# The planner's buffer numbers for conversion blocks, and no conversion beside the first units' thirds

## The chip, the cores and the metric

The kernel runs on one core of one Trainium2 chip, as one launch. The metric is the device time of that launch in microseconds (us). Inside the core five engines work in parallel, each in the order of its own queue: TensorE (PE, matrix products), VectorE (DVE), ScalarE (ACT), GpSimd (POOL) and SyncE (SP, which only issues transfers here). An engine whose next instruction must wait for a semaphore holds up everything behind it in its queue.

## The reference

Three layers follow each other on 2,304 tokens (4 batches of 576) with 512 features.

```python
# 1. attention in a sliding window of 64, 4 batches x 8 heads x 576 x 64
scores = where(0 <= i - j < 64, q @ k.T / 8, -1e9)
x = softmax(scores) @ v                       # -> (2304, 512)
# 2. eight experts; tokens are dealt out greedily by logit, 288 to an expert
order = np.argsort(-(x @ w_gate).flatten())
for idx in order:
    tok, e = divmod(idx, 8)
    if assigned[tok] < 0 and counts[e] < 288:
        assigned[tok] = e; counts[e] += 1
for e in range(8):
    out[assigned == e] = relu(x[assigned == e] @ w1[e]) @ w2[e]   # 512 -> 1024 -> 512
# 3. output network, 512 -> 2048 -> 512
h = out @ w_in
return maximum(0.01 * h, h) @ w_out
```

The inputs of the third layer, w_in and w_out, reach the chip as 32 blocks of 128 x 512 numbers of eight bytes each (512 KB a block), and the kernel itself rebuilds four-byte numbers from them.

## The kernel before, in words

**Stages.** The attention comes first (18 chunks of 128 tokens). Then the greedy dealing is done by a radix search in eight phases (class Router): each phase finds the tokens of one expert in a run of rounds. In a round TensorE counts with small matmuls into the tile rp, VectorE makes r_sat, and from the next rp it makes r_G and r_E for the following round. When a phase has its tokens (`ids`), GpSimd gathers their rows into xg, TensorE transposes them (tile xtp), and they are copied to xT and xF.

**Units.** The experts and the output network are one sequence of units, `Moe.seq`: expert 0, expert 1, output stage 0, experts 2 and 3, output stage 1, and so on. An expert has 8 units of 128 hidden features (units 0 to 7 are expert 0, 8 to 15 expert 1), an output stage has 16 (units 16 to 31 are the first). A unit i is made in two steps. `hstep(i)` is the product h, then ACT's relu into the tile hh. `ystep(i)` is the product with the second matrix, ya for an expert and oa for an output stage. The loop in `Moe.run` (lines 1153 on) queues hstep(i + 1) ahead of ystep(i). Expert 0 works straight from the loaded weights w_raw in float32; later units use weights split in two parts (a high part, cast by ACT, and a low part, by VectorE or GpSimd).

**The first units.** Expert 0's tokens come in three groups of 96. So that TensorE can begin before all have arrived, the products h0 and h1 are made by thirds: `third(i, a)` is 16 matmuls of 128 x 96 in four groups of four. After the third groups, `R.tick()` lets the driver of the routing queue more work. Only then is `hstep(0)` called, which finds all 12 groups done and queues the relu of h0.

**Conversion blocks.** Class Convert turns the 32 blocks into weights. A block is loaded by SP (or, once, by GpSimd) into the tile cv_in, which has four buffers: block n uses the buffer of block n − 4. So its transfer waits until block n − 4 has been used up. The first 18 blocks take three ACT passes and one step on VectorE, the *join*; the others two and two. A block that is kept on the chip is then cast by ACT into res, and VectorE makes its low part there.

**What sets the order.** All instructions are put into the queues by the program in one fixed order that a planner works out as the kernel is built. Class Clocks has a clock for each engine; Engine.call charges each instruction to it (so most operations after the attention have one line in the profile, L1303 before and L1309 after the change). A charged instruction starts when its inputs are written and when its output's buffer is free, and `Clocks.slot` says which buffer a tile lies in. `RouteDriver.tick` and `Convert.acts` and `piece` then ask these clocks whether a routing step or a conversion step fits. `Convert.there(n)` lets a block's first pass be queued once the planner thinks the block landed 400 ns ago. While `quiet` is set, neither passes nor joins are queued; `until(n)` still queues them when a weight is called for.

**The numbers of buffers.** The program's pool really gives block n buffer n mod 4. `Clocks.slot` numbers tiles of a kind in the order in which it meets them:

```python
k = self.ntag.get(t.tag, 0)
self.ntag[t.tag] = k + 1
self.slots[t.name] = t.tag, k % t.tag_meta.bufs
```

The clocks only start after the attention. They meet block 4 first (number 0), then 5, 6 and 3 (numbers 1, 2 and 3); then block 7, which is given number 0, and block 8, number 1. Block 7's transfer is thus charged as if it waited for block 4's buffer, where the pool has it wait for block 3's.

Of the kernel before, what the change touches and what calls it, by code (L numbers as in the profile page):

```python
# [1 line left out]

# [611 lines left out]
def make_pow2(nc, pool):  # L614
    out = []
    for r, (s, n) in enumerate(zip((25,) + SHIFTS, (127,) + NB)):
        w = pool.tile([128, 128], BF, name=f"pow2_{r}", tag=f"pow2_{r}")
        nc.gpsimd.memset(w, 0.0)
        a = 0 if n > 32 else 96
        nc.gpsimd.memset(w[a:a + n], float(1 << s))  # L620
        out.append(w)
    return out
# [30 lines left out]
class Convert:  # L653
# [24 lines left out]
            return self.st[n][:, :, 1].bitcast(F32)  # L678
        return self.pool.tile([128, 512], F32, tag="cv_r", name=f"cv_r{n}", bufs=NRING)
    def there(self, n):  # L680
        return self.done_at(self.st[n]) + 400 <= self.now()
    def open(self, n):

        if n not in self.out:
            while n not in self.st:
                self.load()
            self.out[n], self.left[n] = self.room(n), [2, 1, 0] if n < BYACT else [1, 0]
        t, o, act = self.st[n], self.out[n], self.nc.scalar.activation
        half = t.rearrange("p a b -> p (a b)").bitcast(F16).rearrange("p (a b) -> p a b", b=4)
        k = self.left[n].pop()  # L690
        if k == 0:
            act(o, t[:, :, 1].bitcast(F32), AF.Copy, scale=float(2.0 ** -112))
        elif k == 1:
            act(t[:, :, 0], t.bitcast(U8)[:, :, 3], AF.Copy, scale=1 / 32, bias=-31 / 64)
        else:
            act(half[:, :, 1], o, AF.Copy)
# [107 lines left out]
class Moe:  # L804
# [280 lines left out]
    def run(self):  # L1085
        nc, seq, R = self.nc, self.seq, self.route
        n = len(seq)
# [28 lines left out]
        self.split(0, 0)  # L1116
        self.split(1, 0)
        self.split(0, 1)
        def third(i, a):
            if a == 0:  # L1120
                self.ph[i] = self.pp.tile([128, 512], F32, tag="h", name=f"h{i}")
                self.hdone[i] = 12
            for k in range(4):
                nc.tensor.matmul(self.ph[i][:, 96 * a:96 * a + 96], self.w[i, 0][:, 128 * k:128 * k + 128], self.xF[a][:, k], start=(k == 0), stop=(k == 3), skip_group_check=True)
        for a in range(3):
            R.until(nc.done(self.xg[0, a]))
            self.xtrans(0, a)
            if a < 2:
                third(a, 0)
        for i, a in ((0, 1), (1, 1), (0, 2), (1, 2)):  # L1130
            third(i, a)
            R.tick()
        self.hstep(0)
        self.split(2, 0)
        self.split(1, 1)
        for i in range(n):
# [77 lines left out]
class Clocks:  # L1214
# [11 lines left out]
    def slot(self, ap):  # L1226

        t = ap.tensor
        if not hasattr(t, "tag_meta"):
            return None  # L1230
        if t.name not in self.slots:
            k = self.ntag.get(t.tag, 0)
            self.ntag[t.tag] = k + 1
            self.slots[t.name] = t.tag, k % t.tag_meta.bufs
        return self.slots[t.name]
    def cost(self, e, name, out, ins):
# [150 lines left out]
def build(nc, tc, qT, kT, v, vT, wg, cfd, cid, cbd, w12, wio, out):  # L1387
    with ExitStack() as ctx:
        ctx.enter_context(tc.manual_schedule())
        c = ctx.enter_context(tc.tile_pool(name="c", bufs=1))  # L1390
        dr = ctx.enter_context(tc.tile_pool(name="dr", bufs=1, space=bass.MemoryType.DRAM))
        iwg = c.tile([128, 256], F32, name="iwg")
        ident = iwg[:, :128]
        cft = c.tile([128, CFN], F32, name="cft")
        cit = c.tile([128, CIN], I32, name="cit")
        cbt = c.tile([128, CBN - MW - 128], BF, name="cbt")
        cf = {k: cft[:, o:o + n] for k, (o, n) in CFO.items()}
        ci = {k: cit[:, o:o + n] for k, (o, n) in CIO.items()}
        cb = {k: cbt[:, o - MW - 128:o - MW - 128 + n] for k, (o, n) in CBO.items() if o > MW}
        ones = c.tile([128, 128], BF, name="ones"); nc.vector.memset(ones, 1.0)  # L1400

        nc.scalar.activation(iwg[:, 0:1], ones[:, 0:1], AF.Exp)
        L = c.tile([128, 160], F32, name="L")[:, :NT * 8].rearrange("p (c e) -> p c e", e=8)
        xd = dr.tile([NTOK, DM], F32, name="xd")
        res = [c.tile([128, 2, 512], F32R, name=f"res_{n}") for n in range(NRES)]
        wsp = dr.tile([32 - NRES, 128, 1024], F32, name="wsp")
        cvp = ctx.enter_context(tc.tile_pool(name="cvp", bufs=1))
        cv = Convert(nc, cvp, wio, res)
        slow = cv.spare(CVA)
        def filler(i):  # L1410
            if i == -1:
                for _ in range(3):
                    cv.open(CVA)
                return
            if i is None:
                for _ in slow:
                    pass
                drain()
                return
            if queue and not next(queue[0], False):  # L1420
                queue.pop(0)
            if i == CV0:
                for _ in range(CVL):
                    cv.load()
            if i >= CV0 + 6:
                next(slow, None)
        rp = ctx.enter_context(tc.tile_pool(name="rp", bufs=1))
        rt = Router(nc, rp, None, L, cf, ci, cb, ones, make_pow2(nc, rp))
        rt.ident = ident
        ahead = {5: (0, 6), 11: (6, 12), 14: (12, 15), 17: (15, 18)}  # L1430
        queue = []
        def done(c):
            if c == 4:
                rt.start2()
            if c in ahead:
                queue.append(rt.ahead(*ahead[c]))
            if c == NT - 1:
                drain()
        def drain():
            while queue:  # L1440
                list(queue.pop(0))
        with tc.tile_pool(name="mk", bufs=1) as mk:
            maskb = mk.tile([128, MW + 128], BF, name="maskb")
            nc.scalar.dma_start(maskb, cbd[:, :MW + 128].bitcast(BF))
            wg_sb = iwg[:, 128:].rearrange("p (u e) -> p u e", u=4)
            def early():
                nc.scalar.dma_start(iwg, wg)
            def late():
                nc.sync.dma_start(cit, cid)
                nc.sync.dma_start(cft, cfd)  # L1450
                nc.sync.dma_start(cbt, cbd[:, MW + 128:].bitcast(BF))
                rt.start()
            attention(nc, tc, ident, maskb[:, MW:], qT, kT, v, vT, wg_sb, maskb, xd, L, filler, early, late, done)
        pa = ctx.enter_context(tc.tile_pool(name="m_pa", bufs=4, space=PSUM, reuse_waits="tile"))
        rt.pp = ctx.enter_context(tc.tile_pool(name="rps", bufs=1, space=PSUM, reuse_waits="tile"))
        pm = ctx.enter_context(tc.tile_pool(name="pm", bufs=1, space=PSUM, reuse_waits="tile"))
        rt.p0 = pm
        ph = ctx.enter_context(tc.tile_pool(name="m_ph", bufs=2, space=PSUM, reuse_waits="tile"))
        nc = cv.nc = rt.nc = Clocks(nc)
        nc.at["scalar"] = 7000.0  # L1460
        cv.side = nc.scalar.copy, nc.vector
        cv.now = lambda: max(nc.at["tensor"], nc.at["vector"])
        R = RouteDriver(nc, rt, cv)
        m = Moe(nc, tc, ctx, ident, pm, pa, ph, w12, wsp, xd, out, R)
        cv.relief = R.relief
        m.conv, m.warm = cv, cbt[:, :512]
        m.run()
# [25 lines left out]
```

## Time and profile before

| | us |
|---|---|
| device time, three runs | 774.66, 775.33, 775.5 |
| their median | 775.33 |
| the profiled execution: device time | 770.33 |
| the profiled execution: span of the trace | 768.7 |
| busy TensorE (PE) | 732.2 (95% of the span) |
| busy VectorE (DVE) | 440.3 (57%) |
| busy ScalarE (ACT) | 337.1 (44%) |
| busy GpSimd (POOL) | 165.6 (22%) |

The profile is of one execution, whose own device time is 770.33 us; the span runs from its first to its last recorded instruction. Times in the rows are us from the span's start. PE is TensorE's matmuls, PEld its loading of weights, which overlaps them. "[6.26 <-DMA cv_in<-in_wio_dram]" behind an instruction is the idle time of its engine before it and what ended it. SPq is SP's queue: an instruction there that lasts long is a transfer whose issue waits. In names of tiles the numbers are left out, so cv_in is any conversion block.

### The profile page before, as it was taken

What the parts mean: (1) busy time and instruction counts of PE and PEld (TensorE: products, weight loads), DVE (VectorE), ACT (ScalarE), POOL (GpSimd) and SP (SyncE); (2) the same over time, 40 slices, a digit from 0 to 9 for tenths busy, and PEclk for the clock granted to TensorE, in tenths of its full rate; (3) what the DMA queues carried; (4) which work ended last, traced back from release to release, by engine and by line L of the source; (5) the groups of instructions that cost most, each with busy time, mean ns of one, the idle gap of its engine ahead of it and who ended that gap; (6) DMA issues with size and microseconds to landing.
All of it is one profiled execution on the core that took longest, in us unless ns stands there. A gap on an engine that the chain in (4) does not pass through costs nothing.

```text
span 768.7 us, 14869 instructions
## 1 busy us (share of the span) xinstructions
PE 732.2 (95%) x5706; PEld 619.1 (81%) x5706; DVE 440.3 (57%) x1124; ACT 337.1 (44%) x761; POOL 165.6 (22%) x260
## 2 busy tenths in 40 slices
PE   6989567999999999999999999999999999999996
PEld 4767445798777799987777899888889998888895
DVE  3798884988998797875847823322233222222332
ACT  5898705577866444522122445222234532121321
POOL 6353130410100033010000288000038830000201
PEclk9999768999999999999999999999999999999999
DMA  9996156643785655261324363532436462324652
GB/s 358 416 416 260 49 192 222 201 161 110 253 290 213 237 198 187 84 251 55 132 88 165 105 214 131 216 109 86 163 108 224 138 219 82 110 87 162 245 184 91
DMA packets 39800, 138.55 MB, mean 180 GB/s; under 512 B 4783, under 2 KB 5679, under 8 KB 39729
## 3 DMA queue, kind: packets, MB, share of 16 engines
q1 hardware_dynamic: 34992, 122.62, 44.6%
q0 software_dynamic: 4448, 14.69, 5.5%
q8 instruction: 45, 0.74, 0.4%
q10 hardware_dynamic: 288, 0.30, 0.1%
q14 instruction: 27, 0.21, 0.1%
HBM read 117.66 MB, written 19.92 MB: 179 GB/s over the span
## 4 chain that ended last, share of the span: by engine, by line
PE 89%; DVE 7%; DMA 1%; ACT 1%; issue 1%; POOLq 0%; POOL 0%; SPq 0%; DVEq 0%; ACTq 0%
PE h L1303 39%; PE oa L1303 26%; PE ya L1303 14%; PE rp L1303 2%; PE ao L165 2%; PE as L130 1%; PE apt L150 1%; DVE amx L137 1%; PE xtp L1303 1%; DVE r_G L1303 1%; DMA cv_in<-in_wio_dram 1%; DMA aq<-in_q_dram 1%; PE warm L1303 1%; PE rq L1303 1%; ACT ap L145 1%
## 5 line engine op out<-in xcount | busy, mean ns | idle before, releaser
L1303 PE MATMUL h<-Y,w 128*128 128x512 f32 (+1 forms) x600 | 135.6, 372 | 0.0
L1303 PE MATMUL oa<-w,hh 128*128 128x512 f32 x540 | 134.9, 394 | 0.0
L1303 DVE SCALAR_TENSOR_TENSOR h<-h,tg 128x512 f32<-128x512 f32 (+1 forms) x80 | 51.5, 644 | 127.5 <-ACT tg L1303 127.2
L1303 PEld LDWEIGHTS h<-Y,w 128*128 128x128 f32 x600 | 104.0, 189 | 18.5
L1303 ACT COPY tg<-h 128x512 f32<-128x512 f32 (+1 forms) x80 | 43.7, 546 | 169.9 <-PE h L1303 160.1
L1303 PEld LDWEIGHTS oa<-w,hh 128*128 128x128 f32 x540 | 99.1, 188 | 19.5
L1303 PE MATMUL ya<-hh,w 128*128 128x288 f32 x672 | 101.0, 297 | 0.0
L1303 PE MATMUL h<-xT,w 128*128 128x288 f32 x672 | 100.8, 298 | 0.0
L1303 PEld LDWEIGHTS h<-xT,w 128*128 128x128 f32 x672 | 92.7, 188 | 0.6
L1303 PEld LDWEIGHTS ya<-hh,w 128*128 128x128 f32 x672 | 92.2, 188 | 0.0
L1303 POOL DMA_INDIRECT out_dram<-ot,sidx x18 | 18.9, 1050 | 310.0 <-DVE ot L1303 134.7
L1303 PE MATMUL h<-Y,res 128*128 128x512 f32 (+1 forms) x360 | 83.4, 375 | 0.0
L1303 PE MATMUL oa<-res,hh 128*128 128x512 f32 x324 | 82.3, 399 | 0.2 <-ACT hh L1303 0.2
L1303 POOL TENSOR_TENSOR w<-raw,w 128x512 fp32r<-128x512 f32 x48 | 60.4, 1295 | 95.4 <-ACT w L1303 95.0
L1303 DVE TENSOR_TENSOR hh<-h,hh 128x512 fp32r<-128x512 f32 (+1 forms) x80 | 51.0, 637 | 36.4 <-ACT hh L1303 33.5
L1303 PEld LDWEIGHTS h<-Y,res 128*128 128x128 f32 x360 | 62.3, 188 | 11.9
L1303 ACT CAST hh<-h 128x512 fp32r<-128x512 f32 (+1 forms) x80 | 43.6, 544 | 63.0 <-DVE h L1303 63.0
L1303 PEld LDWEIGHTS oa<-res,hh 128*128 128x128 f32 x324 | 59.4, 188 | 13.9 <-ACT hh L1303 1.2
L1303 ACT ACTIVATE hh<-h 128x288 fp32r<-128x288 f32 (+1 forms) x64 | 26.2, 411 | 87.9 <-PE h L1303 86.8
L1303 ACT CAST w<-raw 128x512 fp32r<-128x512 f32 x112 | 64.1, 621 | 0.0
L1303 DVE SCALAR_TENSOR_TENSOR hh<-h,hh 128x288 fp32r<-128x288 f32 x56 | 25.5, 456 | 64.5 <-ACT hh L1303 64.3
L1303 POOL DMA_INDIRECT xg<-xd,r_ids x24 | 24.1, 1005 | 127.5 <-issue 48.6
(181 smaller groups left out, 961.4 us busy)
## 6 DMA issues: line engine op xcount, KB each, us to landing
w<-wsp SPq DMA_DIRECT2D x80, 512.0 KB, 3.6
raw<-in_w_dram SPq DMA_DIRECT2D x53, 512.0 KB, 4.0
cv_in<-in_wio_dram SPq DMA_DIRECT2D x31, 512.0 KB, 4.5
wsp<-w SPq DMA_DIRECT2D x20, 512.0 KB, 3.1
avo<-in_v_dram SPq DMA_DIRECT2D x6, 876.0 KB, 9.8
aq<-in_q_dram SPq DMA_DIRECT2D x12, 384.0 KB, 9.7
avt<-in_vt_dram SPq DMA_DIRECT2D x6, 768.0 KB, 9.5
xd<-ax SPq DMA_DIRECT2D x18, 256.0 KB, 6.6
```

The source lines that it names most:

```text
L130: nc.tensor.matmul(S[64 * t:64 * t + 64, a, u, :].rearrange("p (b c) -> p b c", b=2), q[h], k[h], start=False, stop=True, skip_group_check ...
L137: nc.vector.tensor_reduce(out=mx, in_=S[:, a:a + n], axis=AX.X, op=ALU.max)
L145: nc.scalar.activation(p[:, u, :], S[:, a, u, :], AF.Exp, bias=nm[a][:, u:u + 1], scale=0.125)
L150: nc.tensor.transpose(pt[:, u, :], p[:, u, :], ident)
L165: nc.tensor.matmul(o[64 * t:64 * t + 64, h // 4, h % 4, :], ptb[:, u, 64 * t:64 * t + 64], (ve, vo)[t][m][:, s, h, :], start=True, stop=Tr ...
L1303: return f(*a, **kw)
```

## The change

The change has three parts. First, `Clocks.slot` takes a block's buffer from the number in its name, and at the start meets the tiles of the blocks already opened, so that they count. Second, `quiet` is set before the thirds of units 0 and 1 and is taken back after `hstep(0)`: in between no pass, no join and no load of a block is queued. Third, `there(n)` asks 4,000 ns in place of 400 for block 7 alone. No instruction's form changes; the rest of the order follows from the planner.

```diff
+import re
...
     def there(self, n):
-        return self.done_at(self.st[n]) + 400 <= self.now()
+        return self.done_at(self.st[n]) + (4000 if n == 7 else 400) <= self.now()
...
         self.split(0, 1)
+        self.conv.quiet = True
         def third(i, a):
...
             third(i, a)
             R.tick()
         self.hstep(0)
+        self.conv.quiet = False
         self.split(2, 0)
...
             k = self.ntag.get(t.tag, 0)
-            self.ntag[t.tag] = k + 1
+            m = re.match(r"cv_in(\d+)_", t.name)
+            if m:
+                k = int(m[1])
+            self.ntag[t.tag] = max(self.ntag.get(t.tag, 0), k + 1)
             self.slots[t.name] = t.tag, k % t.tag_meta.bufs
...
         nc = cv.nc = rt.nc = Clocks(nc)
+        for k in sorted(cv.out):
+            nc.slot(cv.out[k])
         nc.at["scalar"] = 7000.0
```

**ACT at the relus of units 0 and 1.** These are ACT's instructions from the copies of expert 0's tokens on; hh0 is the relu of unit 0, and `cv_r7<-cv_in7` is the first pass of conversion block 7. Before:

```order
L1303 COPY xT0_1_2188<-xtp0_0_2189 128x384
L1303 COPY xF1_2209<-xtp0_1_2204 128x384
L1303 COPY xT0_0_2187<-xtp0_2_2237 128x384
L1303 ACTIVATE cv_r7_2253<-cv_in7_2248 128x512
L1303 ACTIVATE hh0_2271<-h0_2196 128x288
L1303 ACTIVATE hh1_2273<-h1_2212 128x288
L1303 CAST res_2_73<-cv_in4_1190 128x512
L1303 ACTIVATE cv_r6_2301<-cv_in6_2132 128x512
L1303 CAST res_3_74<-cv_in5_1193 128x512
L1303 ACTIVATE cv_in6_2132<-cv_in6_2132 128x512
L1303 ACTIVATE cv_in6_2132<-cv_r6_2301 128x512
L1303 ACTIVATE hh2_2353<-h2_2313 128x288
```

And now:

```order
L1309 COPY xT0_1_2188<-xtp0_0_2189 128x384
L1309 COPY xF1_2209<-xtp0_1_2204 128x384
L1309 COPY xT0_0_2187<-xtp0_2_2237 128x384
L1309 ACTIVATE hh0_2288<-h0_2196 128x288
L1309 ACTIVATE hh1_2290<-h1_2212 128x288
L1309 ACTIVATE cv_r6_2322<-cv_in6_2132 128x512
L1309 ACTIVATE cv_in6_2132<-cv_in6_2132 128x512
L1309 ACTIVATE cv_in6_2132<-cv_r6_2322 128x512
L1309 CAST res_2_73<-cv_in4_1190 128x512
L1309 ACTIVATE hh2_2368<-h2_2334 128x288
L1309 CAST res_3_74<-cv_in5_1193 128x512
L1309 ACTIVATE cv_r7_2437<-cv_in7_2327 128x512
```

The first pass of block 7 stood ahead of hh0 and now stands behind hh2 and the cast res_3; hh0 and hh1 follow the copies directly. The other two passes of block 7 come with it, and block 6's three passes now stand ahead of the cast res_2.

**VectorE beside the thirds and the first products of expert 0.** These are VectorE's steps behind the last copy of expert 0's tokens, into the rounds of the search for expert 1; cv_r3, cv_in4 and cv_in5 as outputs are the joins of blocks 3, 4 and 5, and res_2 and res_3 low parts. Before:

```order
L1303 SCALAR_TENSOR_TENSOR cv_r3_1778<-cv_r3_1778,cv_in3_1006 128x512
L1303 SCALAR_TENSOR_TENSOR r_sat_126<-rp16_2217,ones_66 127x8
L1303 SCALAR_TENSOR_TENSOR cv_in4_1190<-cv_in4_1190 128x512
L1303 SCALAR_TENSOR_TENSOR r_G1_128<-r_E_1_0_2202,rp17_2251,cft_63 128x18x31
L1303 SCALAR_TENSOR_TENSOR r_E_1_1_2265<-r_E_1_0_2202,rp17_2251,r_M_122 128x18
L1303 SCALAR_TENSOR_TENSOR cv_in5_1193<-cv_in5_1193 128x512
L1303 SCALAR_TENSOR_TENSOR r_sat_126<-rp18_2280,ones_66 31x8
L1303 SCALAR_TENSOR_TENSOR r_G0_127<-r_E_1_1_2265,rp19_2306,cft_63 128x18x31
L1303 SCALAR_TENSOR_TENSOR r_E_1_2_2310<-r_E_1_1_2265,rp19_2306,r_M_122 128x18
L1303 TENSOR_TENSOR res_2_73<-cv_in4_1190,res_2_73 128x512
L1303 TENSOR_TENSOR res_3_74<-cv_in5_1193,res_3_74 128x512
L1303 SCALAR_TENSOR_TENSOR r_sat_126<-rp20_2315,ones_66 31x8
```

And now:

```order
L1309 SCALAR_TENSOR_TENSOR r_sat_126<-rp16_2217,ones_66 127x8
L1309 SCALAR_TENSOR_TENSOR r_G1_128<-r_E_1_0_2202,rp17_2248,cft_63 128x18x31
L1309 SCALAR_TENSOR_TENSOR r_E_1_1_2255<-r_E_1_0_2202,rp17_2248,r_M_122 128x18
L1309 SCALAR_TENSOR_TENSOR r_sat_126<-rp18_2261,ones_66 31x8
L1309 SCALAR_TENSOR_TENSOR r_G0_127<-r_E_1_1_2255,rp19_2286,cft_63 128x18x31
L1309 SCALAR_TENSOR_TENSOR r_E_1_2_2298<-r_E_1_1_2255,rp19_2286,r_M_122 128x18
L1309 SCALAR_TENSOR_TENSOR cv_r3_1778<-cv_r3_1778,cv_in3_1006 128x512
L1309 SCALAR_TENSOR_TENSOR cv_in4_1190<-cv_in4_1190 128x512
L1309 SCALAR_TENSOR_TENSOR r_sat_126<-rp20_2302,ones_66 31x8
L1309 SCALAR_TENSOR_TENSOR r_G1_128<-r_E_1_2_2298,rp21_2332,cft_63 128x18x31
L1309 SCALAR_TENSOR_TENSOR r_E_1_3_2337<-r_E_1_2_2298,rp21_2332,r_M_122 128x18
L1309 TENSOR_TENSOR res_2_73<-cv_in4_1190,res_2_73 128x512
```

The joins of blocks 3 and 4 moved behind two rounds of the search (r_sat, r_G, r_E), to the place after r_E_1_2, and the join of block 5 one round further. The load of block 7 is queued on SP behind the join of block 3, and moves with it.

## Rows read from the trace of the kernel before

**Rows 1.** The page: the span and the busy time of the engines.

```profile
span 768.7 us, 14869 instructions
...
PE 732.2 (95%) x5706; PEld 619.1 (81%) x5706; DVE 440.3 (57%) x1124; ACT 337.1 (44%) x761; POOL 165.6 (22%) x260
```

**Rows 2.** Waits of TensorE: engine, tile, line, releaser; us in total, times, longest.

```profile
PE rp L1303 <- DVE r_OB L1303: 4.8, 1, 4.8
PE ya L1303 <- ACT hh L1303: 4.1, 1, 4.1
...
PE oa L1303 <- ACT hh L1303: 0.2, 1, 0.2
```

**Rows 3.** The chain that ended last, 110 to 126 us: start, us, what.

```profile
112.37 6.76 DMA cv_in<-in_wio_dram
...
119.71 0.40 ACT hh L1303
```

**Rows 4.** Timeline, 111 to 131 us: start, us, engine, what, idle before and releaser.

```profile
112.37 18.85 SPq L1303 DMA_DIRECT2D cv_in<-in_wio_dram  x5
...
114.08 1.95 PE L1303 MATMUL h<-xT,w_raw 128*128 128x96 f32 x16
...
119.15 0.66 ACT L1303 ACTIVATE cv_r<-cv_in 128x512 f32<-128x512 f32 x1 [6.26 <-DMA cv_in<-in_wio_dram]
...
120.16 1.33 PE L1303 MATMUL ya<-hh,w_raw 128*128 128x288 f32 x2 [4.12 <-ACT hh L1303]
```

**Rows 5.** Busy time in stretches: us, PE, PEld, DVE, ACT, POOL, clock, DMA share, GB/s.

```profile
118.00:120.00 2.00, 0.00 (x0) 0.00 (x0) 0.00 (x0) 0.85 (x2) 0.00 (x0) 0.50 1.02 418
...
122.00:124.00 2.00, 2.00 (x5) 1.35 (x6) 0.97 (x3) 1.95 (x3) 0.00 (x0) 0.50 0.00 0
...
126.00:128.00 2.00, 2.00 (x10) 1.42 (x10) 1.49 (x4) 0.27 (x1) 0.00 (x0) 1.00 0.88 334
```

**Rows 6.** Timeline of TensorE: the starts of h2, ya of unit 1, h3.

```profile
124.92 0.65 PE L1303 MATMUL h<-xT,w_raw 128*128 128x288 f32 x2
...
127.53 0.65 PE L1303 MATMUL ya<-hh,w_raw 128*128 128x288 f32 x2
...
130.15 0.65 PE L1303 MATMUL h<-xT,w_raw 128*128 128x288 f32 x2
```

**Rows 7.** Timeline of one routing round, TensorE and VectorE.

```profile
126.45 0.17 PE L1303 MATMUL rp<-r_sat,pow 128*128 128x8 bf16 x1
...
126.69 0.81 DVE L1303 SCALAR_TENSOR_TENSOR r_G<-r_E,rp,cft 128x558 bf16<-128x558 f32 x1 [0.45 <-PE rp L1303]
...
127.56 0.69 DVE L1303 SCALAR_TENSOR_TENSOR cv_r<-cv_r,cv_in 128x512 int32<-128x512 int32 x1
...
128.68 0.18 DVE L1303 TENSOR_TENSOR_SCAN r_sat<-rp,ones 31x8 bf16<-31x8 f32 x1 [0.43 <-PE rp L1303]
...
129.07 0.17 PE L1303 MATMUL rp<-r_sat,pow 128*128 128x8 bf16 x1
```

**Rows 8.** Tile cv_in, 85 to 140 us: ns min/median/max by operation; load to landing.

```profile
L1303 ACT ACTIVATE cv_in<-cv_in x15: 649/708/1382, 89.3 to 136.6; 128x512 int32<-128x512 uint8 x7, 128x512 f32<-128x512 f32 x4, 128x512 f16<-128x512 f32 x4
...
DMA to landing us min/median/max: 3.4/3.5/6.8
```

**Rows 9.** Tile w_raw, issued by POOL from 108.3 to 108.6 us.

```profile
L1303 POOL DMA_DIRECT2D w_raw<-in_w_dram x1: 594/594/594, 108.4 to 108.4; - x1
...
DMA to landing us min/median/max: 6.2/6.2/6.2
```

**Rows 10.** Busy time in two stretches (columns as in rows 5).

```profile
114.90:122.00 7.10, 2.98 (x33) 2.34 (x32) 0.00 (x1) 2.85 (x7) 0.00 (x0) 0.71 0.81 329
184.00:281.00 97.00, 96.97 (x528) 76.23 (x527) 85.88 (x203) 59.12 (x110) 4.06 (x6) 1.00 0.64 223
```

**Rows 11.** Timeline, 286 to 304 us: gather of routing phase 3, its transposes.

```profile
288.45 0.92 POOL L1303 DMA_INDIRECT xg<-xd,r_ids  x1 [0.30 <-issue]
...
303.34 0.82 PE L1303 MATMUL xtp<-iwg,xg 96*128 96x96 f32 x8
```

## The prediction

> **What bounds the kernel now.** Four views were read, from coarse to fine. The page gives the span and TensorE's share: 768.7 us, TensorE busy for 95% of it [rows 1]. So what TensorE waits for is nearly all that can be won, and the list of its waits is next. There two waits stand out after the attention stage [rows 2]: 4.8 us behind r_OB, inside routing phase 0, which the change does not touch, and 4.1 us of the product ya behind ACT's hh, once. The chain of waits tells where the second comes from [rows 3]: over 112.37 to 119.13 us the end of the program hangs on one DMA into cv_in, a conversion block, not on anything that ya needs. The timeline shows the mechanism [rows 4]: TensorE ends the last thirds of h1 at 114.08 + 1.95 = 116.03 us; ACT's next instruction is not the relu of h0 but the first pass of conversion block 7, which waits 6.26 us for that DMA; the relu stands behind it on the same queue, and ya starts at 120.16 us. [...]
>
> **The change, step by step.** The sum is made against the profiled execution, 770.33 us; the median of the runs shown, 775.33 us, lies 5.0 us above it, and I carry that distance over.
>
> 1. *The wait goes.* In the new order of ACT both relus, hh0 and hh1, stand directly behind the copy of xT, and block 7 behind hh2. The 16 passes of 1.95 us are the last thirds of h0 and h1, 8 each [rows 4], so h0 is complete near 115.06 us, and its relu (0.40 us of chain, from 119.71 to ya at 120.16) ends near 115.6. ya follows TensorE's own work without a wait: −4.1 us. One routing group of 19 small matmuls now stands between the two thirds and no longer inside ya; the same work, earlier, and VectorE, which feeds it, was through with its steps by 114.9 us [rows 10]. Nothing is charged.
>
> 2. *The slow clock goes.* ya of unit 0 with its routing group took 124.92 − 120.16 = 4.76 us at the low level [rows 4, 6]; the same set for unit 1 took 130.15 − 127.53 = 2.62 us at the full one [rows 6]. Without the idle stretch the first runs like the second: −2.1 us. Bounds: 0 if the clock falls all the same, 2.1 if it stays up.
>
> 3. *Conversion moves later on VectorE.* The joins of blocks 3, 4 and 5 stood before or just after 114 us, between routing steps, where VectorE then sat idle; they now fall into the routing rounds that run beside ya and h2. A round of TensorE is 129.07 − 126.45 = 2.62 us, from one small matmul on r_sat to the next [rows 7]. In it VectorE needs 0.24 us until r_G starts, 127.56 − 126.69 = 0.87 for r_G and r_E, 0.69 for one join, and then r_sat; with one join it had 0.43 us to spare. Three of the new rounds hold two conversion steps each. r_sat then starts at 126.69 + 0.87 + 2 x 0.69 = 128.94 in place of 128.68, ends at 129.12, and TensorE's matmul comes about 0.1 us late. Three rounds: +0.3 us. Bounds: 0 (the rounds have other lengths; the second has one product more) and 3 x 0.69 = 2.1, if each second step lies wholly open.
>
> 4. *Block 7 itself.* Its load still waits for the join of block 3, which now ends near 116.5 + 0.24 + 0.87 + 0.69 = 118.3 us. It lands 3.5 us later if it is alone (the median), near 121.9, and 6.8 us later, near 125.2, if it meets the expert weights again (the maximum, which is this very load) [rows 8]. ACT comes to block 7 after hh2 and a cast, near 122.8 us: h2 ends two rounds after 116.5, at 121.7, then 0.4 and 0.65. Three passes each of blocks 7 and 8 (0.65 + 0.7 + 1.38 = 2.7 us a block [rows 8]) stand before hh3, which is then ready near 128.6 us, or 131.0 with the late landing. ya needs it after h4, near 119.1 + 4 x 2.62 + 2.1 = 131.7 us. So the cover is 3.1 us, or 0.7: nothing is charged, and what is late next is hh3.
>
> 5. *Weights needed earlier.* h2 starts near 119.1 instead of 124.92 us. Its weights were issued at 108.4 us and landed 6.2 us later, at 114.6 [rows 9]. Covered by 4.5 us.
>
> 6. *The rest of the program.* The right buffer numbers reorder conversions, routing steps and weight casts through all later stages. TensorE's only wait there is 0.2 us, of oa on hh [rows 2]. VectorE is the tight engine: busy 85.88 of 97 us in the first output stage, units 16 to 31 of the sequence [rows 10]. It lost the idle stretch of 114.9 to 122.0 us, about 7 us with nothing on it [rows 10], and took over three joins (3 x 0.69 = 2.1 us). Its idle time in the 97 us is 11.1 us, so that fits; the order up to the first expert of routing phase 1 is otherwise nearly unchanged, with one join fewer ahead of it. The gathers of the expert of routing phase 3 come two units later in the order, and they were issued by 289.4 us for transposes at 303.3 us [rows 11]. Nothing is charged, with a chance kept for it below.
>
> The sum: −4.1 − 2.1 + 0.3 = −5.9 us; 770.33 becomes 764.4 in its own execution, and 775.33 becomes **769.4 us**.
>
> [...] The one trace here shows the low level once after this idle stretch and cannot tell how often.
>
> **The rivals.**
> *A. The clock gives nothing.* The timed runs do not pay the slow stretch before, or pay one like it after. For it: the profiled run is 5.0 us below the median, so timed runs differ from it in something. Against it: in the trace the low level follows the idle stretch by 2 us and ends 4.6 us into the work. −4.1 + 0.3 = −3.8: 771.5 us.
> *B. A new wait takes part of the place.* The routing rounds lose the whole 2.1 us of step 3, or hh3 comes late because block 7 lands late and block 8 queues behind it. −5.9 + 1.8 = −4.1, or with both that and up to 1.5 us of hh3, −2.6: 771.2 to 772.7 us.
> *C. Slower: a conversion block is missing in the first output stage.* VectorE starts that stage with its lost 7 us still open. If a block is not joined when its weights are called for, the driver queues it whole at that place and TensorE waits for all of it: 3.5 us of load, 2.7 of passes, 0.65 for a cast like a pass, 0.69 each for join and low part [rows 7, 8], 8.2 us. It decides when the backlog is over the 11.1 us that VectorE had idle there [rows 10]; 9.2 us (7.1 + 2.1) is near that, though routing steps can give way. −5.9 + 8.2 = +2.3: 777.6 us. Against it: TensorE waits for no such block now, and in the new order the low parts of hh in that stage stand behind no more VectorE work than before.
> *D. The relu is held all the same,* by another instruction on ACT, so that the change does not do what it says: 775.3 us. Against it: only copies that ran before 113 us stand ahead of it now.
>
> **How the numbers follow.** The forecast has 0.70, A 0.13, B 0.08, C 0.05, D 0.04. A measurement of this kernel can tell about 0.2% (1.55 us) from no change, so faster means below 773.8 us. Faster: forecast, A and B, 0.91; same: D, 0.04; slower: C, 0.05. The range: downward, no new round wait at all gives −6.2 (769.1), and the runs shown lie up to 0.7 us below their median: 768.4, taken as 768.2. Upward it takes in A and B with the middle of their stretch, to 772.3. Forecast, A and most of B lie in it.
>
> **What would show each step right or wrong.** Right: the wait of ya on hh falls from 4.1 to under 0.3 us; the chain no longer names cv_in between 110 and 125 us; the granted clock is 1.00 from 108 us to the end; two or three waits of TensorE on r_sat of 0.1 us each come in; the first output stage starts near 178 instead of 184 us, and all later stages are shifted by the same amount. Wrong: a granted clock of 0.50 within 116 to 125 us would refute step 2; waits of ya on hh at a later unit would be block 7 again; a wait of h or oa on res or w between 178 and 275 us would be rival C; a shift that shrinks from stage to stage would mean that the reordering of step 6 is not free.

## The result and the profile after

| device time, us | before | changed |
|---|---|---|
| median of five runs | 774.66 | 767.52 |
| lowest to highest | 773.75 to 775.5 | 766.61 to 769.66 |
| the profiled execution (span) | 770.33 (768.7) | 767.52 (765.9) |

The ratio is 0.9911, with a 95% interval of 0.9892 to 0.9929: the change wins 7.1 us, where 5.9 were forecast (0.9924, inside this interval, but outside those of the two later comparisons below). The forecast time, 769.4 us, is 1.9 us too high, and the measured time lies 0.7 us below the range. Of the 1.9 us, 0.7 are the baseline: the forecast started from a median of 775.33, and over five runs it is 774.66. The other 1.2 us are a gain that the forecast did not have. Timed twice more beside the kernel before, on two chips, the same change won 7.0 us (764.38 against 771.33, ratio 0.9908, 0.9895 to 0.9922) and 7.3 us (764.36 against 771.70, ratio 0.9899, 0.9885 to 0.9913), so the size is no accident of one comparison.

The two profiled executions are only 2.8 us apart. That is the first puzzle, and it is why more profiles of both kernels were taken.

The page after, for [rows 1]:

```profile
span 765.9 us, 14862 instructions
...
PE 730.6 (95%) x5705; PEld 618.8 (81%) x5706; DVE 442.6 (58%) x1128; ACT 337.6 (44%) x761; POOL 163.6 (21%) x256
```

The waits of TensorE after, for [rows 2] (engine, tile, line, releaser; us in total, times, longest):

```profile
PE rp L1309 <- DVE r_OB L1309: 5.7, 2, 4.8
...
PE rp L1309 <- DVE r_sat L1309: 2.5, 6, 1.2
...
PE rp L1309 <- DVE r_ip L1309: 1.2, 2, 0.8
...
PE oa L1309 <- ACT hh L1309: 0.5, 1, 0.5
```

The wait of ya on hh, 4.1 us before, is gone. But r_OB is waited for twice now, 5.7 us in place of 4.8, and r_ip and hh come with 0.8 and 0.5 us at their longest. The 1.2 us for r_sat lie at 94.69 us, in routing phase 0, ahead of anything that the change moves.

The timeline after, 113.5 to 126.5 us, for [rows 4, 6]:

```profile
115.43 1.06 PE L1309 MATMUL h<-xT,w_raw 128*128 128x96 f32 x8
...
116.52 0.41 ACT L1309 ACTIVATE hh<-h 128x288 f32<-128x288 f32 x1 [2.28 <-PE h L1309]
...
116.80 1.11 PE L1309 MATMUL h<-xT,w_raw 128*128 128x96 f32 x8
...
117.78 1.70 PE L1309 MATMUL ya<-hh,w_raw 128*128 128x288 f32 x6
...
119.57 6.69 SPq L1309 DMA_DIRECT2D cv_in<-in_wio_dram  x4
...
120.44 1.70 PE L1309 MATMUL h<-xT,w_raw 128*128 128x288 f32 x6
...
125.27 0.69 ACT L1309 ACTIVATE cv_r<-cv_in 128x512 f32<-128x512 f32 x1 [1.08 <-DMA cv_in<-in_wio_dram]
```

ACT makes the relu of h0 at 116.52 us, as soon as h0's last third is done, and ya starts at 117.78 straight behind the thirds of h1, with no idle time. The load of block 7 is issued at 119.57 us, and ACT waits for it until 125.27 us; now nothing of TensorE's hangs on that.

Windows after, for [rows 5] (us, PE, PEld, DVE, ACT, POOL, clock, DMA share, GB/s):

```profile
118.00:120.00 2.00, 2.00 (x26) 1.59 (x26) 2.00 (x4) 1.96 (x4) 0.00 (x0) 1.00 1.05 426
...
122.00:124.00 2.00, 2.00 (x27) 1.65 (x26) 1.22 (x4) 0.78 (x2) 0.00 (x0) 1.00 0.50 182
```

The granted clock stays at 1.00 where it was 0.50, from 118 to 124 us.

**Where the time goes, over twelve profiles.** Four points of each timeline are compared: A, the first product h; B, the first ya; C, the start of h2; D, the start of ya of unit 5; the end is the start of the last matmul of the last product oa. (us, each worked out from the starts of these rows; the kernels are those of the experiments below.)

| profile | A | A to B | B to C | C to D | D to end | A to end |
|---|---|---|---|---|---|---|
| before | 109.18 | 10.98 | 4.76 | 20.95 | 615.05 | 651.74 |
| e1_before | 108.59 | 11.49 | 4.36 | 20.95 | 615.76 | 652.56 |
| e10_before | 109.17 | 10.77 | 4.74 | 20.95 | 615.67 | 652.13 |
| e4_warm18 | 109.40 | 12.35 | 2.72 | 21.00 | 615.79 | 651.86 |
| e2_quiet | 109.90 | 7.26 | 2.66 | 22.12 | 616.03 | 648.07 |
| e3_slot | 109.59 | 7.39 | 3.15 | 21.96 | 619.48 | 651.99 |
| e6_qacts | 108.40 | 7.26 | 2.59 | 20.70 | 615.04 | 645.59 |
| changed | 110.52 | 7.26 | 2.66 | 20.51 | 617.20 | 647.63 |
| e5_after | 109.84 | 7.26 | 2.66 | 20.40 | 615.04 | 645.36 |
| e9_after | 109.83 | 7.26 | 2.66 | 20.40 | 615.01 | 645.33 |
| e7_hold12 | 109.01 | 11.89 | 4.30 | 20.40 | 615.43 | 652.03 |
| e8_hold12w | 108.94 | 11.89 | 2.64 | 20.40 | 615.18 | 650.11 |

The puzzle resolves in three columns. Point A, before which the change moves no instruction, differs by up to 2 us between executions (108.40 to 110.52), and the first profile after had the latest. From D to the end that profile lost 2.2 us against the other two of the same kernel. And the first profile before was the quickest of three there. So the first pair shows too little: from A to the end the two later profiles of the changed kernel are 6.4 to 7.2 us shorter than the three before. Whole profiled executions differ less, by 6.0 and 6.2 us (764.58 and 764.54 against 770.56 and 770.70), since A came 0.7 to 1.3 us later in these two of the changed kernel; that is taken as chance here, as e7 and e8, with the same order up to A, have it at 109.01 and 108.94 us.

### The profile page after: what moved, and what is told of

It reads as the page before. It is cut to its first block, busy times and chain, and to the rows that moved or that the text cites. A ratio compares the mean times of both kernels' runs of the same rounds, so it can differ in the third digit from the quotient of the medians.

```text
span 765.9 us, 14862 instructions
## 1 busy us (share of the span) xinstructions
PE 730.6 (95%) x5705; PEld 618.8 (81%) x5706; DVE 442.6 (58%) x1128; ACT 337.6 (44%) x761; POOL 163.6 (21%) x256
## 4 chain that ended last, share of the span: by engine, by line
PE 88%; DVE 7%; DMA 2%; issue 1%; ACT 1%; POOLq 0%; POOL 0%; SPq 0%; DVEq 0%; ACTq 0%
PE h L1309 39%; PE oa L1309 26%; PE ya L1309 13%; PE rp L1309 2%; PE ao L166 1%; DVE amx L138 1%; PE apt L151 1%; DMA avt<-in_vt_dram 1%; PE xtp L1309 1%; DVE r_G L1309 1%; DMA iwg<-in_wg_dram 1%; PE as L131 1%; PE rq L1309 1%; PE warm L1309 1%; DVE ax L182 0%
## 5 line engine op out<-in xcount | busy, mean ns | idle before, releaser
L1309 POOL TENSOR_TENSOR w<-raw,w 128x512 fp32r<-128x512 f32 x44 | 55.4, 1290 | 97.2 <-ACT w L1309 92.0
```

What stands on the lines that cost most here:

```text
L1309: return f(*a, **kw)
```

## The experiments

Theory: the gain is the wait for block 7's load and the low clock behind it, each worth what the prediction says, and the timed runs pay them in full. Rivals: the clock costs nothing in timed runs; the wait alone is larger than the trace shows; the gain comes from the order of the later stages.

### e1 and e10: the kernel before again

No edit. What was expected of the first:

> The kernel before, unchanged, profiled a second time. It asks why the timed runs lie at 774 to 775 us and the execution of the profile at 770.3. Theory 1 (the 4.3 us lie outside the changed stretch): the wait of ya on hh is again 4.1 us (within 0.5) and the low clock again ends within 5 us of ya's start; if this execution is near 774, the 4 us are found before the first product h (109.18 us in the first profile) or after unit 8. Theory 2 (the 4.3 us lie in the changed stretch, so that the change wins more in the timed runs than the first profile shows): the execution is near 774 us, and the stretch from the first product h to the second unit's ya (18.35 us in the first profile) is 3 to 5 us longer, by a longer wait for the conversion block's load or a longer low clock. Timed against itself: within 0.2%.

and of the second:

> The kernel before, a third profile: how long the load of block 7 holds ya. The first two show 4.1 and 4.6 us, and the run with matmuls in the wait 5.4 us. If the wait varies with the transfer: between 4 and 6 us again, and the low clock ends 3 to 5 us after ya starts; if it is fixed near 4.1 us, the 7 us of the change need another source.

Measured: 771.26 us, ratio 0.9999 (0.9991 to 1.0008), and on another chip 771.00 against 771.70, ratio 0.9989 (0.9977 to 1.0001). Two rows of the waits of TensorE in e1, and then in e10:

```profile
PE ya L1303 <- ACT hh L1303: 4.6, 1, 4.6
...
PE rp L1303 <- DVE r_E L1303: 0.6, 1, 0.6
```

```profile
PE ya L1303 <- ACT hh L1303: 3.9, 1, 3.9
...
PE rp L1303 <- DVE r_sat L1303: 2.1, 7, 0.5
```

The wait of ya is 4.1, 4.6 and 3.9 us in three profiles. It follows the transfer: block 7's load, issued at 111.8 to 112.4 us, landed after 6.76, 7.27 and 6.54 us, each time 2.6 us more than the wait. Issued at 111.6 to 112.8 us in e3, e4 and e6 it took 7.9, 8.1 and 8.1 us, so the wait of the first profile lies at the short end of what the load can cause; how long the load is in the runs that were only timed, nothing shows. But the stretch did not grow by 3 us: theory 2 of the first text, that the changed stretch is 3 to 5 us longer, fell. What the first profile before did not show is the second row of each: 0.6 us for r_E in e1, and in e10 one wait of r_sat of 0.5 us that was not there (7 waits in place of 6). Both lie in the first output stage, at 228.7 and 224.55 us. The first profile had no such wait from 130 us on, only the 0.2 us of oa on hh.

### e5 and e9: the changed kernel again

No edit. Expected:

> The changed kernel, unchanged, again, beside the kernel before on one chip. From the first product h to the last product oa the first profile of the change is 4.1 us shorter than the first profile before and 4.9 us shorter than the second; the timed medians differed by 7.1 us. Theory 1 (the profiles show the whole gain; the 7.1 us hold some 3 us of another chip or another start of the run): 4 to 5 us faster than before here, about 766.3 to 767.3 us where before is 771.3. Theory 2 (timed runs pay more for the wait and the low clock than the profiles): 7 us faster again, about 764 us. In its profile the three late waits (r_ip 0.8, hh 0.5, r_OB 0.9 us) come back in both theories, if they belong to the order and not to one run.

> The changed kernel on the chip of the two holds, as their zero: 6 to 8 us faster than before, as on the other chip; ya of unit 0 without a wait; the later waits on r_ip and r_OB there or not, from 0.3 to 2 us in all.

Measured: 764.38 and 764.36 us, 7.0 and 7.3 us faster than before. Theory 1 of e5, 4 to 5 us, fell, and its theory 2 gave the size, but its reason, that timed runs pay more for the same wait and the same clock, is not shown: of the 6.7 us that e7's profile is longer than e9's from A to the end, its timed runs pay 6.0. The waits of e9:

```profile
PE rp L1309 <- DVE r_OB L1309: 4.8, 1, 4.8
...
PE rp L1309 <- DVE r_sat L1309: 1.6, 6, 0.3
...
PE oa L1309 <- ACT hh L1309: 0.5, 1, 0.5
...
PE rp L1309 <- DVE r_ip L1309: 0.3, 1, 0.3
```

The second wait on r_OB (0.9 us) and most of that on r_ip are there neither in e9 nor in e5: they belonged to one execution. The 0.5 us of oa on hh came in every profile with this later order.

### e2: only the stop of conversion

```diff
         self.split(0, 1)
+        self.conv.quiet = True
...
         self.hstep(0)
+        self.conv.quiet = False
```

> Only the second part of the change: no conversion from the thirds to the first relu; buffer numbers as before. Both relus then stand free of block 7, whose three passes stand ahead of hh2 instead of behind it, and nothing changes later than expert 0. If the gain is the wait and the clock, and the later loss of 2.1 us in the profile after (waits of 0.8 us near 280 us, 0.5 near 339, 0.9 near 444) comes from the reordering by the buffer numbers: faster than before by 5.5 to 6.3 us less a wait of ya for hh2 of 0 to 1 us, none of the three later waits, and 1 to 2 us faster than the full change. Rival (the buffer numbers are needed: block 7's load now holds hh2 as it held hh0): a wait of ya on hh of 2 to 4 us at unit 2, the low clock again, and less than half of the gain.

Measured: 768.25 us against 771.26, ratio 0.9967 (0.9956 to 0.9978): 3.0 us, less than half of the gain. A to B and B to C are those of the changed kernel, so the wait and the clock are won in full. The loss is elsewhere. The timeline of e2, 122 to 129 us:

```profile
122.75 0.67 ACT L1305 ACTIVATE cv_r<-cv_in 128x512 f32<-128x512 f32 x1 [1.97 <-DMA cv_in<-in_wio_dram]
...
125.52 0.65 ACT L1305 CAST res<-cv_in 128x512 fp32r<-128x512 f32 x1
...
126.20 0.69 DVE L1305 TENSOR_TENSOR res<-cv_in,res 128x512 fp32r<-128x512 f32 x1 [2.11 <-ACT res L1305]
...
127.52 0.18 DVE L1305 TENSOR_TENSOR_SCAN r_sat<-rp,ones 31x8 bf16<-31x8 f32 x1
127.75 0.17 PE L1305 MATMUL rp<-r_sat,pow 128*128 128x8 bf16 x1 [1.60 <-DVE r_sat L1305]
```

ACT waits 1.97 us for block 7's load; its passes and hh2 stand ahead of the cast of res_3; the low part of res_3 waits 2.11 us on VectorE for that cast; r_sat stands behind it; and TensorE waits 1.60 us for r_sat. So the same transfer reaches TensorE by another way, through the queues of ACT and VectorE, and not by hh2, as the rival had it. From D on e2, whose later order is that of the kernel before, is 1.0 us slower than the later profiles of the changed kernel, 0.64 of it a wait for r_E at 225.52 us, as in e1. The spread of its runs is 3.8 us (766.91 to 770.71); that of the changed kernel is 0.8 and 0.6 us in e5 and e9, though 3.1 in the first comparison. The two losses, 1.6 and 1.0 us, explain 2.6 of the 2.8 us between the profiled executions (767.35 and 764.58), but not the 4.0 us between e2's gain and the full one: e2's other runs are mostly slower than the one that was profiled (median 768.25), and why is not shown.

### e3: only the buffer numbers

```diff
+            m = re.match(r"cv_in(\d+)_", t.name)
+            if m:
+                k = int(m[1])
...
+        for k in sorted(cv.out):
+            nc.slot(cv.out[k])
```

> Only the first part: the right buffer numbers, conversion not stopped. Block 7 now stands behind hh1, but the three passes of block 6 (2.7 us) stand ahead of hh0. If the numbers are what frees the relu: block 6 has landed when ACT comes to it at 112.9, its passes end at 115.6 us, when h0 is just done; ya waits at most 0.7 us, the clock stays up, and the gain is 5 to 6 us less the later loss of some 2 us: 3 to 4 us faster in its profile. Rival (stopping conversion is what frees it): block 6 lands late or its passes do, ya waits 2 us or more, and the gain is under 2 us.

Measured: 768.66 us, ratio 0.9968 (0.9955 to 0.9981): 2.6 us faster. The rival fell: block 6 had landed, and ya did not wait for hh (A to B 7.39 us). The timeline of e3, 112 to 125 and 146 to 150 us:

```profile
120.73 0.67 ACT L1307 ACTIVATE cv_r<-cv_in 128x512 f32<-128x512 f32 x1 [2.75 <-DMA cv_in<-in_wio_dram]
...
124.33 0.17 PE L1307 MATMUL rp<-r_sat,pow 128*128 128x8 bf16 x1 [1.45 <-DVE r_sat L1307]
```

```profile
147.88 0.55 PE L1307 MATMUL xtp<-iwg,xg 96*128 96x96 f32 x4 [1.74 <-DMA xg<-xd,r_ids]
...
148.77 0.52 PE L1307 MATMUL xtp<-iwg,xg 96*128 96x96 f32 x4 [0.35 <-DMA xg<-xd,r_ids]
```

Block 7's load landed at 120.7 us and came to TensorE through r_sat again (1.45 us); and in this order expert 1's transposes wait for their gathers, 1.74 and 0.35 us. Behind these two waits the granted clock falls again, from 149.9 to 153.3 us:

```profile
150.00:152.00 2.00, 2.00 (x6) 1.34 (x5) 2.00 (x5) 1.97 (x3) 1.83 (x5) 0.50 0.52 211
```

The two waits and this stretch take most of the 4.4 us by which e3 is longer than the changed kernel from D to the end (619.48 against 615.04). The execution profiled here is the slowest of e3's eight runs (770.96, median 768.66), so the later waits need not be in the others. So each of the first two parts alone wins the first wait, and each leaves block 7 where it holds something else. Of these two parts it takes both to put block 7 behind hh2 and the cast of res_3; e6 below gets there by another edit.

The order of the built kernels tells two things more, for which nothing was timed. The third part, the 4,000 ns, moves nothing: without it the order is the same on every engine. And with the stop in place it is the number of block 7 alone that moves the rest, including the whole later order.

### e4: matmuls in the wait, on the kernel before

```diff
         self.hstep(0)
+        wt2 = self.pa.tile([128, 512], F32, tag="acc", name="warm2", bufs=4)
+        for _ in range(18):
+            nc.nc.tensor.matmul(wt2, self.warm[:, :128], self.warm, start=True, stop=True)
         self.split(2, 0)
```

> The kernel before with 18 more matmuls of 128 x 512 on a spare tile (3.9 us at the full clock), put on TensorE between the last thirds and the first ya, so that TensorE is busy while it waits for hh; nothing else changes. If the low clock from 118 to 124.8 us comes of the idle stretch: the wait of ya on hh is gone in name only (ya starts no earlier), the granted clock is 1.00 through 116 to 126 us, and the run is 2.1 us faster than before. If the clock costs nothing in the runs that are timed, or falls all the same: no change (within 0.7 us), or slower by what of the 3.9 us stands after the relu.

Measured: 770.10 us against 771.26, ratio 0.9983 (0.9974 to 0.9992): 1.2 us faster, with a matmul stream added. The timeline and two windows of e4:

```profile
116.31 3.83 PE L1136 MATMUL warm<-cbt 128*128 128x512 bf16 x17
...
121.75 0.75 PE L1306 MATMUL ya<-hh,w_raw 128*128 128x288 f32 x2 [1.61 <-ACT hh L1306]
```

```profile
118.00:120.00 2.00, 2.00 (x10) 0.78 (x8) 0.00 (x0) 0.00 (x0) 0.00 (x0) 1.00 0.91 361
...
122.00:124.00 2.00, 2.00 (x27) 1.50 (x27) 0.55 (x2) 2.00 (x5) 0.00 (x0) 1.00 0.00 0
```

The load came late in this execution, the slowest of the eleven (TensorE was filled for 3.83 us by the 17 matmuls that the trace has, and still waited 1.61), so ya started later than in any profile before; but the clock stayed at 1.00 and B to C is 2.72 us, not 4.76. The gain of 1.2 us has an interval of 0.6 to 2.0 us: less than the 2.1 us expected, and why is open. But rival A, that the clock gives nothing, is out.

### e6: only ACT's passes stopped

```diff
+        self.qa = False
...
-        while self.now() and not self.quiet and self.nc.at["scalar"] <= self.now() + ASLACK:
+        while self.now() and not self.quiet and not self.qa and self.nc.at["scalar"] <= self.now() + ASLACK:
...
         self.split(0, 1)
+        self.conv.qa = True
...
         self.hstep(0)
+        self.conv.qa = False
```

> Before with only ACT's passes stopped from the thirds to the first relu: the joins of blocks 3, 4 and 5 stay where they were, in VectorE's idle time, and block 7's load is issued near 112.4 us as before; buffer numbers as before. Both relus stand free; block 7's first two passes stand ahead of hh2, and the later order is nearly that of the full change. If step 3 of the prediction was right (the moved joins cost 0.3 us) and the later loss belongs to the later order: within 0.6 us of the full change, with the three late waits again. Rival 1 (the moved joins cost up to 2.1 us, in rounds of TensorE that wait for r_sat): 1 to 2 us faster than the full change. Rival 2 (block 7's load, which lands at 119 to 121 us, now holds hh2): a wait of ya on hh at unit 2, 1 us or more slower than the full change.

Measured: 764.02 us (763.36 to 765.35), beside 764.38 for the changed kernel on the same chip: no difference that can be told. The timeline of e6, 109 to 128 us:

```profile
111.59 11.98 SPq L1306 DMA_DIRECT2D cv_in<-in_wio_dram  x5
...
116.19 1.22 ACT L1306 CAST res<-cv_in 128x512 fp32r<-128x512 f32 x2
...
119.72 0.68 ACT L1306 ACTIVATE cv_r<-cv_in 128x512 f32<-128x512 f32 x1
...
126.89 0.17 PE L1306 MATMUL rp<-r_sat,pow 128*128 128x8 bf16 x1 [0.16 <-DVE r_sat L1306]
```

The joins were in VectorE's idle time here, and block 7's load was issued early, at 111.59 us. ACT makes the casts of res_2 and res_3 first and comes to block 7 at 119.72 us, when the load (8.1 us) has landed; 0.16 us of TensorE's time is all that is waited for r_sat. C to D is 20.70 us, not shorter than the 20.40 to 20.51 of the changed kernel. So a version that leaves the joins where they were wins nothing that can be told, though timed runs cannot tell 0.3 us here. Its later order is the changed kernel's but for some conversion steps up to 158 us, and D to the end is the same. More than was asked is shown: neither the buffer numbers nor the stop of the joins is needed, and this one stop of ACT's passes wins as much as the whole change.

### e7 and e8: the wait put back without the transfer

Both are made on the changed kernel; the first edit is in both.

```diff
+        hd = self.wk.tile([128, 512], F32, name="hold", bufs=1)
+        for _ in range(12):
+            nc.nc.scalar.activation(hd, self.warm, AF.Copy)
         self.hstep(0)
         self.conv.quiet = False
```

and for e8 behind these lines also

```diff
+        wt2 = self.pa.tile([128, 512], F32, tag="acc", name="warm2", bufs=4)
+        for _ in range(18):
+            nc.nc.tensor.matmul(wt2, self.warm[:, :128], self.warm, start=True, stop=True)
```

> The changed kernel with 12 more passes of ACT (128 x 512, on a scratch tile) directly ahead of hh0, so that the relu comes some 4 us late again, now behind work of a fixed length and not behind a transfer; nothing else in the order changes. If the prediction's two terms are right (wait 4.1 and low clock 2.1 us, both paid in the runs that are timed): ya waits 3 to 4.5 us in the profile, the low clock follows for about 5 us, and the run is 5 to 6.5 us slower than the changed kernel, near the kernel before less 0.5 to 2 us, with runs that agree within 1.5 us. If the wait for a transfer is what makes timed runs worse than the profile: the same, and the spread of its runs is clearly smaller than the 3.3 us of the kernel before. If the idle stretch costs only itself: slower by the wait alone, 3 to 4.5 us.

> As the run before (12 passes of ACT ahead of hh0), and 18 matmuls of 128 x 512 on a spare tile on TensorE behind the last thirds, which fill most of the wait. If the low clock comes of the idle stretch and costs 2.1 us: ya starts no earlier, no low clock behind it, 1.5 to 2.1 us faster than the run with the hold alone. If the clock costs nothing in timed runs: the same as the hold alone within 0.5 us.

Measured on one chip: the changed kernel 764.36, e7 770.39 (769.55 to 772.71), e8 768.42 us (767.92 to 769.32), the kernel before 771.70. e7's timeline and windows:

```profile
112.62 7.92 ACT L1137 ACTIVATE hold<-cbt 128x512 f32<-128x512 bf16 x12
...
120.89 3.25 PE L1312 MATMUL ya<-hh,w_raw 128*128 128x288 f32 x6 [4.49 <-ACT hh L1312]
```

```profile
118.00:120.00 2.00, 0.00 (x0) 0.00 (x0) 0.63 (x2) 1.90 (x4) 0.00 (x0) 0.50 0.88 272
122.00:124.00 2.00, 2.00 (x6) 1.23 (x5) 0.00 (x0) 1.97 (x3) 0.00 (x0) 0.50 0.00 0
```

and e8's:

```profile
116.19 4.04 PE L1142 MATMUL warm<-cbt 128*128 128x512 bf16 x18
...
120.83 1.72 PE L1315 MATMUL ya<-hh,w_raw 128*128 128x288 f32 x6 [0.59 <-ACT hh L1315]
```

```profile
118.00:120.00 2.00, 2.00 (x11) 0.80 (x9) 0.56 (x1) 1.90 (x4) 0.00 (x0) 1.00 0.82 246
...
122.00:124.00 2.00, 2.00 (x27) 1.53 (x26) 0.51 (x2) 1.97 (x3) 0.00 (x0) 1.00 0.01 2
```

ya starts at the same time in both (120.89 and 120.83 us), and they are 1.97 us apart: that is the low clock in timed runs, against 2.1 forecast (in the profiles B to C is 4.30 against 2.64 us, and A to the end 1.92 us apart). e8 is 4.06 us slower than the changed kernel: that is a wait of ya by which B comes 4.63 us later in the profile (A to B 11.89 against 7.26). Its length was chosen with the 12 passes, so that it is near the 4.1 us of the forecast says nothing of the transfer's own wait; what it shows is that timed runs pay such a wait nearly in full and not more. Together the hold costs 6.0 us, and e7 is still 1.3 us faster than the kernel before, whose wait it has again (ratio 0.9987, 0.9977 to 0.9997). What is left over no profile places: from A to the end e7 takes 652.03 us, and the three before 651.74 to 652.56. It can lie in the later order, of which the table has 0.2 to 0.3 us from D to the end (e7 against e1 and e10, and nothing against the first profile). It can lie in loads of block 7 that hold ya longer, in the timed runs of the kernel before, than the 12 passes do. And it can be chance: e10's seven runs of the kernel before, on the same chip, have a median of 771.00, 0.6 us above e7. The 0.55 us that it has less in C to D are mostly the routing group of 19 small matmuls that A to B has in its place (114.81 to 115.29 us, 0.48).

The second expectation of e7 fell, and of the first that its runs agree within 1.5 us. The relu stood behind 12 passes of ACT (7.92 us in the profiles of e7 and e8 alike), and the 12 runs still spread over 3.2 us, beside 3.1 for the 22 of the kernel before on this chip (770.18 to 773.25). So a relu that stands behind a transfer is not needed for such a spread. With TensorE kept busy, in e8, the spread is 1.4 us, and the mean granted clock of the runs goes with it, 0.977 to 0.983 in e7 and 0.982 to 0.984 in e8. That the low clock makes the runs differ is likely by this, but not shown: e8 has only 5 runs, e2 spreads over 3.8 us although the clock stayed at 1.00 there in the profile from 116 to 130 us, and the changed kernel's clock goes from 0.981 to 0.985 with times within 0.8 us (e5, e9).

## Why the prediction was wrong

- **Step 1, the wait: right.** Forecast −4.1 us, by the transfer behind which the relu stood. Shown by the timeline after; that timed runs pay such a wait is shown by e8 against the changed kernel (4.06 us for 4.63 in the profile). The price was read from one execution: in three profiles of the kernel before the wait is 3.9 to 4.6 us, and with the longest loads seen (8.1 us, less 2.6) it would be 5.5, an estimate. What timed runs of that kernel wait is not known.
- **Step 2, the clock: right.** Forecast −2.1 us, for the granted clock of 0.50 behind the idle stretch [rows 5]. B to C fell from 4.36 to 4.76 us to 2.66 (−1.7 to −2.1), and e7 against e8 gives 1.97 us in timed runs. Four profiles have the wait for hh without matmuls in it (before, e1, e10, e7), and the granted clock was 0.50 from 118 to 122 us in each; with matmuls in it (e4, e8) it stayed at 1.00. So −3.8, the sum without the clock (rival A), does not hold. How often the low level comes in runs that were only timed is not shown.
- **Step 3, the moved joins: wrong by 0.3 us.** I charged +0.3 us for three rounds with two conversion steps. No wait of TensorE on r_sat came between A and D in the changed kernel, and e6, which leaves the joins in place, is not faster by anything that can be told. The rounds had room for a second step of 0.69 us: in the first profile after, r_sat follows the second step at once three times (120.18, 122.81 and 125.94 us), and TensorE does not wait.
- **Step 4, block 7: right that it costs nothing, for half of the reason.** Its load was issued at 119.57 us, 1.3 us later than forecast (A itself is 1.3 us later in that execution), and landed by 125.27, near the late end that I gave; in the two later profiles it took 3.7 and 4.1 us. hh3 was ready in time. That block 7 can reach TensorE through the cast of res_3, its low part and r_sat, as e2 and e3 show, I did not see. The changed kernel escapes that by the place of the cast.
- **Step 5, the weights: right**; h2 never waited.
- **Step 6, the rest of the program: this is the step that failed.** I charged nothing, and gave it no bound on the side of a gain. The claim that TensorE's only wait there was 0.2 us rested on one profile. Both later profiles of the kernel before show one more wait, of 0.6 and 0.5 us, on routing steps of the first output stage (e4 and e2, with the same later order, show 0.6 too); the new order has none there in its three profiles, and 0.3 us more on hh. From D to the end this is some 0.7 us for two of the three profiles before, and nothing for the first. My own sign for this step, a shift that shrinks from stage to stage, pointed the wrong way: in the first pair the shift falls from 4.9 us at D to 2.8 at the end, by waits that came in that execution alone; against e5 and e9 it stays at 5.7.
- **What makes up the miss.** Without the 0.3 of step 3, and with the 0.7 us of step 6 if most runs have that wait, the sum is −6.9 us, and 7.1, 7.0 and 7.3 were measured. The rest, 0.1 to 0.4 us, is not placed; longer loads of block 7 in the timed runs of the kernel before (step 1) would give it, and so would chance.
- **The rivals.** A fell by e4 and by e7 against e8, D by the timeline after. Of B, later waits of the right size came (2.2 us with those on r_ip, hh and r_OB), but in later stages and all three only in one execution. C did not come: no wait on res or w is in any list of waits.
- **The range.** Its lower end had in it the runs' spread and the 0.3 us of step 3, and nothing for steps 4 to 6. With 0.7 us for a gain in step 6 it would have just held the result. **The carried distance**, 5.0 us between the profile and the timed median, did not hold either: in the later runs, on three chips, the kernel before takes 771.3 to 771.7 us and the changed one, on two of them, 764.4, each some 3 us less than in the first comparison. Most of the distance belonged to that first set of runs.

What stays open: why the r_E and r_sat waits come in most executions and not in the first one; why e2's timed runs are slower than its profiled one; how long the load of block 7 is in runs that were only timed; and how much of the 1.3 us of e7 is that load, how much the later order and how much chance.

## What to carry to other kernels

When an engine waits for a transfer that its own result doesn't need, look one queue further than the wait: the stop and the buffer numbers each freed the relu alone, and the same transfer came back through the queues of ACT and VectorE and a routing step (1.60 us of TensorE's time in e2, 1.45 in e3). And look for the smallest edit: with only ACT's passes stopped (e6) the load went out early (111.59 us, against 119.57), the casts went first, and the whole gain was there. Here a wait that was taken from TensorE was worth half as much again as its length, as the granted clock was 0.50 behind it: 4.06 us for the wait (e8 against the changed kernel) and 1.97 for the clock (e7 against e8). And a list of waits from one execution is a sample: where a change reorders everything behind it, bound its cost on both sides, by a second profile or by the spread of the runs.

## What was not expected of the hardware

The start of expert 0 (point A) differs by 2 us between executions of the same instructions, 108.40 to 110.52 us, and the granted clock goes with it: over 106 to 108 us its mean is 0.91 in e6 and 0.80 in e1, where A comes first (108.40 and 108.59), and 0.50 in the three profiles of the changed kernel (109.83 to 110.52), where it rises only behind 108 us. In e3 the granted clock fell to 0.50 behind two waits of TensorE of 1.74 and 0.35 us; behind one of 1.45 us earlier in e3, and one of 1.60 us in e2, it stayed at 1.00. And with an idle stretch of 4.5 us of TensorE behind the 12 passes of ACT the device times spread over 3.2 us in 12 runs (e7), with the same stretch filled with matmuls over 1.4 in 5 (e8): filling it won 2.0 us (1.2 in e4) with work that no result needs.
